# Attention and two MLPs on one core: each head pair's work put into two phases

## The chip, the cores and the metric

The kernel runs on one core of a Trainium2 chip. A core has five engines that run their own instruction lists in order: TensorE (PE; its weight loads are shown as PEld), VectorE (DVE), ScalarE (ACT), GpSimd (POOL) and SyncE (SP, which here only starts DMA transfers). TensorE writes its results to PSUM, of which this kernel uses eight banks; DVE and ACT read them from there. The metric is the device time of one execution in microseconds (us), lower is better.

## The reference

Attention over 4 batches and 12 heads (448 positions, 64 channels), then a squared-ReLU MLP and a gated MLP, each over 1792 tokens of width 768:

```python
def _attn_ref(q, k, v, g_q, g_k):
    q_n, k_n = (rmsnorm(q, g_q), rmsnorm(k, g_k))
    scores = scale * np.matmul(q_n, k_n.transpose(0, 1, 3, 2))
    scores = scores - np.max(scores, axis=-1, keepdims=True)
    attn = np.exp(scores)
    attn = attn / (np.sum(attn, axis=-1, keepdims=True) + 1e-09)
    return np.matmul(attn, v)
...
    x = attn_out.transpose(0, 2, 1, 3).reshape(B * S, H * D)
    h = np.maximum(x @ w_in, 0.0)          # 768 -> 2048
    x = h * h @ w_out                      # 2048 -> 768
    g = x @ w_gate                         # 768 -> 1536
    return (g / (1 + np.exp(-g)) * (x @ w_val)) @ w_out   # 1536 -> 768
```

The MLP weights come as 64-bit floats. The kernel reads them as pairs of 32-bit words and puts 32-bit floats together from them.

## The kernel before

**Attention** works on 24 pairs of heads. A pair's queries and keys are squared (`square`, ACT), summed (`sumsq`, DVE), turned into reciprocal roots (`rsqrt`) and normalised (`normalise`, POOL). `transposes` turns them on TensorE; ACT takes the high part of each value (L292) and DVE the remainder (`lows`), both into the tile `th`. The two heads of a pair lie in rows 0 to 63 and 64 to 127, so `maxpass` and `scores` are matmuls on 64 rows, one for each head. Positions go in four chunks of 112. `maxpass` multiplies the high parts alone, and DVE reduces the result to a maximum per query (L315). `negmax` transposes the four chunks of maxima into one tile `nm`. `scores` multiplies three times (high with high, high with low, low with high), adds the negative maxima by a fourth matmul, and ACT takes the exponential (L340, tile `p`). POOL adds chunks in pairs (`sg`, L343). `av` multiplies by V, `sums` sums the exponentials. Sums go to SBUF, are laid out anew by DMA (`sp`), inverted (`recip`, DVE), sent through DRAM to all rows (`row`, `rb`, SP), and `xnorm` multiplies the output by them into `x`.

The order is set by a table: each step is entered with a slot and a place in the slot (`at`), pairs are four slots apart, and the list is run sorted. A slot holds one chunk of scores of one pair, one maxpass chunk of a later pair, and whatever else is due. AV comes in two halves. PSUM is cut into three tiles of two banks for transposes, maxima and scores (`ps_s`), one bank for AV (`ps_a`), and one that sums and negmax share (`ps_n`).

**The MLPs** run in units: `up` (one block of 448 tokens, one slab of 128 hidden columns, 18 matmuls), `gateval` (two such) and `down` (36 matmuls). A value x weight product is three matmuls of high and low parts. Weight slabs are prepared step by step (`pieces`, six steps on DVE and ACT for each slab), and `prep(n)` runs n of them; `prep` is called from the attention table too. `split_x` cuts the attention output into high and low parts. `down` of a block follows one unit behind the `up` that ends its hidden block. `drain` holds the last reciprocals and multiplications, run in the first units.

Of the kernel before, what the change touches and what calls it, by code (L numbers as in the profile page):

```python
# [19 lines left out]
def kernel(  # L20
# [66 lines left out]
    state = {"load": 0, "prep": 0, "freed": 0, "half": None, "done": None, "cap": NEARLY}  # L87
# [5 lines left out]
    def load_slab():  # L93
        i = state["load"]
        if i >= len(slabs):
            return
        key, src = slabs[i]
        wide = src.dtype == I32
        if wide:
            t = mem["wraw"].tile([P, KD, 2 * P], I32, tag="raw", name="raw")  # L100
        else:
            t = mem["wraw"].tile([P, KD, P], F32, tag="raw", name="raw")
        nc.sync.dma_start(out=t, in_=src)
        raws[i] = t
        state["load"] += 1

# [6 lines left out]
    def pieces():  # L113
        for i, (key, src) in enumerate(slabs):
# [8 lines left out]
            else:  # L123
# [17 lines left out]
                load_slab()  # L141
# [8 lines left out]
            if raw.dtype != I32:  # L150
                load_slab()
# [15 lines left out]
    def split_x(t, ks=range(KD)):  # L167
        b0, n = blocks[t]
        for kk in ks:
            eng = nc.gpsimd if kk % 3 == 2 else nc.vector  # L170
            split(xs[t][:, 0, kk, :], xs[t][:, 1, kk, :], x[:, kk, b0:b0 + n], eng)

    def attention():
        with ExitStack() as late:
# [21 lines left out]
            mxz = [one_p.tile([CP, NCH, P], F32, tag=f"mxz{i}", name=f"mxz{i}") for i in range(2)]  # L196
# [6 lines left out]
            START = -18  # L203
            raw_t, qk_t, tp_t, xu_t, v_t, th_t, sq_t, ss_t, nm_t, p_t, sg_t, av_t, sp_t, rb_t = ({} for _ in range(14))
# [26 lines left out]
            def square(pi, j=None):  # L231
                if not ok(pi):
                    return
                if pi not in sq_t:
                    sq_t[pi] = nat.tile([CP, 2, NV, D], F32, tag="sq", name="sq")
# [14 lines left out]
            def rsqrt(pi, eng=None):  # L250
# [5 lines left out]
                e.tensor_scalar(out=ms, in0=ms, scalar1=1.0 / D, scalar2=1e-6, op0=ALU.mult, op1=ALU.add)  # L256
                nc.scalar.activation(out=u, in_=ms, func=AF.Ln)
                nc.scalar.activation(out=r, in_=u, func=AF.Exp, scale=-0.5)
                e.tensor_tensor(out=u, in0=r, in1=r, op=ALU.mult)
                e.tensor_tensor(out=u, in0=u, in1=ms, op=ALU.mult)  # L260
                e.tensor_scalar(out=u, in0=u, scalar1=-0.5, scalar2=1.5, op0=ALU.mult, op1=ALU.add)
                e.tensor_tensor(out=r, in0=r, in1=u, op=ALU.mult)
# [18 lines left out]
            def transposes(pi):  # L281
# [3 lines left out]
                th = th_t[pi] = th_p.tile([P, 4, S], F32R, tag="th", name="th")  # L285
                ps = ps_s.tile([P, 2, 512], F32, tag="s", name="s")
                for j in (1, 0):
                    for c in range(NCH):
                        nc.tensor.transpose(ps[:, j, c * CP:(c + 1) * CP], t[:, j, c], ident[:CP, :CP])  # L289
                tp_t[pi] = ps  # L290
                for j, gg, hi in ((1, gk, 0), (0, gq, 3)):
                    nc.scalar.activation(out=th[:, hi, :], in_=ps[:, j, :S], func=AF.Copy, scale=gg[:, 0:1])  # L292

            def lows(pi, j):
                if not ok(pi):
                    return
                ps, th = tp_t[pi], th_t[pi]
                gg, hi, li = ((gq, 3, 2), (gk, 0, 1))[j]
                nc.vector.scalar_tensor_tensor(
                    out=th[:, li, :], in0=ps[:, j, :S], scalar=gg[:, 0:1], in1=th[:, hi, :].bitcast(F32),  # L300
                    op0=ALU.mult, op1=ALU.subtract,
                )
# [3 lines left out]
            def maxpass(pi, c):  # L306
# [3 lines left out]
                ps = ps_s.tile([P, 2, 512], F32, tag="s", name="s")  # L310
# [4 lines left out]
                nc.vector.tensor_reduce(out=mxz[pi % 2][:, c, 0:P:D], in_=ps[:CP, :, :S], op=ALU.max, axis=AX.X)  # L315

            def negmax(pi):
                if not ok(pi):
                    return
                ps = ps_n.tile([P, 512], F32, tag="n", name="n")  # L320
                for c in range(NCH):
                    nc.tensor.transpose(ps[:, c * CP:(c + 1) * CP], mxz[pi % 2][:, c, :], ident[:CP, :CP])  # L322
                nm = nm_t[pi] = one_p.tile([P, S], F32R, tag="nm", name="nm", bufs=2)
                nc.scalar.activation(out=nm, in_=ps[:, :S], func=AF.Copy, scale=-1.0)

            def scores(pi, c):
# [3 lines left out]
                ps = ps_s.tile([P, 2, 512], F32, tag="s", name="s")  # L330
# [10 lines left out]
                if c % 2 == 1:  # L341
                    sg = sg_t[pi, c // 2] = p_p.tile([CP, 2, S], F32, tag="sg", name="sg", bufs=4)
                    nc.gpsimd.tensor_tensor(out=sg, in0=p_t[pi, c - 1], in1=p, op=ALU.add)  # L343


            def av(pi, c):
                if not ok(pi):
                    return
                if c == 0:
                    av_t[pi] = ps_a.tile([P, 512], F32, tag="av", name="av")  # L350
                p = p_t.pop((pi, c))
                for a, s in halves:
                    nc.tensor.matmul(  # L353
                        av_t[pi][s, :S], v_t[pi][:, a, c * D:(c + 1) * D], p[:, a, :],
                        start=(c == 0), stop=(c == NCH - 1),
                    )
                if c == NCH - 1:
# [276 lines left out]
```

## Time and profile before

| what | us |
|---|---|
| median of three runs (lowest, highest) | 1290.71 (1289.81, 1294.98) |
| the profiled execution | 1289.78 |
| its span, first to last instruction | 1288.0 |
| PE busy | 1264.1 (98%) |
| DVE, ACT, POOL busy | 820.5 (64%), 433.3 (34%), 288.4 (22%) |

The busy shares are means over two unlike halves: attention up to about 273 us, then the MLPs. A busy time on PE is the time with a matmul under way; matmuls overlap by their pipeline, so the cost of a block of matmuls is read from its start to the start of the next, not from its duration. An idle time in brackets behind a row is that of the engine just before it, with what ended it.

### The profile page before, as it was taken

How to read it: one execution, taken by the hardware profiler on the slowest of the kernel's cores; microseconds unless marked ns; L12 is line 12 of the kernel's file. 1: busy time of each engine (PE TensorE's matmuls, PEld its weight loads, DVE VectorE, ACT ScalarE, POOL GpSimd, SP SyncE). 2: the span in 40 equal slices, each digit the busy share in tenths (PEclk: the TensorE clock that was granted, in tenths of full speed). 3: DMA queues.
4: the chain of work that ended last, by engine and by line, in shares of the span. 5: the costliest groups of instructions: out<-in, count | busy, mean ns of one | idle time of the engine just before them, and what ended most of it. 6: DMA issues, size and time to landing. Idle time of an engine off the chain costs nothing.

```text
span 1288.0 us, 16575 instructions
## 1 busy us (share of the span) xinstructions
PE 1264.1 (98%) x6720; PEld 1059.1 (82%) x6720; DVE 820.5 (64%) x1151; ACT 433.3 (34%) x677; POOL 288.4 (22%) x258
## 2 busy tenths in 40 slices
PE   6999999999999999999999999999999999999998
PEld 3555555568989889898989899999999999999998
DVE  7777887766656565656565667475565664764634
ACT  5767777642322231313132442122121121221210
POOL 4666777632111120202020560000000000000000
PEclk9999999999999999999999999999999999999999
DMA  6233332130211121212021112021111120220013
GB/s 169 74 111 89 104 105 72 49 99 25 74 50 54 48 71 50 65 34 74 25 74 50 50 50 74 23 77 50 49 49 50 50 74 25 74 74 25 25 44 129
DMA packets 64830, 82.35 MB, mean 64 GB/s; under 512 B 8176, under 2 KB 61168, under 8 KB 64752
## 3 DMA queue, kind: packets, MB, share of 16 engines
q1 hardware_dynamic: 64752, 81.28, 20.1%
q8 instruction: 53, 0.87, 0.3%
q14 instruction: 25, 0.20, 0.0%
HBM read 75.50 MB, written 5.59 MB: 63 GB/s over the span
## 4 chain that ended last, share of the span: by engine, by line
PE 65%; issue 26%; POOL 6%; DVE 1%; ACT 1%; SPq 0%; DMA 0%; POOLq 0%; ACTq 0%
PE ps L499 29%; PE ps L547 17%; PE s L338 7%; PE av L353 6%; POOL s L521 5%; PE s L312 2%; PE s L289 2%; PE n L369 2%; PE n L322 1%; DMA raw<-in_q_dram 0%; SPq L220 0%; DVE mxz L315 0%; POOL sg L343 0%; DVE bits L134 0%; DVE hid L165 0%
## 5 line engine op out<-in xcount | busy, mean ns | idle before, releaser
L499 PE MATMUL ps<-xs,w 128*128 128x448 f32 x2880 | 599.8, 368 | 1.6 <-ACT sb L373 1.6
L499 PEld LDWEIGHTS ps<-xs,w 128*128 128x128 f32 x2880 | 542.5, 188 | 50.3 <-ACT sb L373 2.4
L547 PE MATMUL ps<-hid,w 128*128 128x448 f32 x2016 | 423.5, 367 | 5.8 <-ACT hid L164 3.2
L547 PEld LDWEIGHTS ps<-hid,w 128*128 128x128 f32 x2016 | 379.4, 189 | 41.2 <-ACT hid L164 6.2
L555 DVE TENSOR_TENSOR xacc<-ps,xacc 128x448 f32<-128x448 f32 x288 | 165.7, 617 | 47.7 <-PE ps L547 47.6
L165 DVE TENSOR_TENSOR hid<-s,hid 128x448 fp32r<-128x448 f32 x112 | 70.0, 625 | 157.8 <-ACT hid L164 157.6
L521 POOL TENSOR_TENSOR s<-s 128x448 f32<-128x448 f32 x64 | 76.0, 1188 | 364.0 <-ACT s L520 361.2
L164 ACT CAST hid<-s 128x448 fp32r<-128x448 f32 x112 | 63.5, 567 | 247.6 <-DVE s L534 159.4
L315 DVE TENSOR_REDUCE mxz<-s 112x2 f32<-112x896 f32 x96 | 103.8, 1084 | 34.5 <-PE s L312 34.2
L343 POOL TENSOR_TENSOR sg<-p 112x896 f32<-112x896 f32 x48 | 103.3, 2152 | 57.6 <-ACT p L340 57.6
L147 ACT CAST w<-bits 128x768 fp32r<-128x768 f32 x68 | 56.7, 834 | 156.6 <-DVE bits L143 156.6
L340 ACT ACTIVATE p<-s 112x896 f32<-112x896 f32 x96 | 86.7, 916 | 45.5 <-PE s L338 43.9
L338 PEld LDWEIGHTS s<-th 64*112 64x112 f32 x576 | 45.3, 174 | 54.9 <-issue 33.7
L149 DVE TENSOR_TENSOR w<-bits,w 128x768 fp32r<-128x768 f32 x68 | 65.7, 967 | 37.4 <-ACT w L147 36.2
L338 PE MATMUL s<-th 64*112 64x448 f32 x576 | 82.2, 391 | 0.9 <-ACT p L340 0.9
L353 PE MATMUL av<-p,v 112*64 112x448 f32 x384 | 82.8, 552 | 0.0
L530 ACT ACTIVATE s<-ps 128x448 f32<-128x448 f32 x48 | 26.1, 543 | 164.7 <-PE ps L499 164.7
L520 ACT ACTIVATE s<-ps 128x448 f32<-128x448 f32 x64 | 34.4, 538 | 132.9 <-PE ps L499 132.9
L132 ACT ACTIVATE w<-raw 128x768 fp32r<-128x768 f32 x68 | 61.5, 905 | 45.4 <-PE ps L547 45.4
L138 DVE SCALAR_TENSOR_TENSOR bits<-raw,bits 128x768 int32<-128x768 int32 x68 | 75.2, 1106 | 2.3
L531 DVE TENSOR_TENSOR s<-ps,s 128x448 f32<-128x448 f32 x48 | 29.8, 622 | 72.5 <-ACT s L530 72.5
L534 DVE TENSOR_TENSOR s<-ps,s 128x448 f32<-128x448 f32 x48 | 30.0, 624 | 71.9 <-PE ps L499 71.0
(56 smaller groups left out, 781.2 us busy)
## 6 DMA issues: line engine op xcount, KB each, us to landing
raw<-in_moe_w_out_dram SPq DMA_DIRECT2D x28, 768.0 KB
raw<-in_moe_w_in_dram SPq DMA_DIRECT2D x16, 768.0 KB
raw<-in_moe_w_gate_dram SPq DMA_DIRECT2D x12, 768.0 KB
raw<-in_moe_w_val_dram SPq DMA_DIRECT2D x12, 768.0 KB
raw<-in_k_dram SPq DMA_DIRECT2D x24, 224.0 KB
raw<-in_q_dram SPq DMA_DIRECT2D x24, 224.0 KB
v<-in_v_dram SPq DMA_DIRECT2D x24, 224.0 KB
rb<-row SPq DMA_DIRECT2D x48, 112.0 KB
```

The source lines that it names most:

```text
L138: nc.vector.scalar_tensor_tensor(out=bits, in0=lo, scalar=29, in1=bits, op0=ALU.logical_shift_right, op1=ALU.bitwise_or)
L149: nc.vector.tensor_tensor(out=t[:, 1, :], in0=src, in1=t[:, 0, :].bitcast(F32), op=ALU.subtract)
L165: (eng or nc.vector).tensor_tensor(out=dl, in0=src, in1=dh.bitcast(F32), op=ALU.subtract)
L315: nc.vector.tensor_reduce(out=mxz[pi % 2][:, c, 0:P:D], in_=ps[:CP, :, :S], op=ALU.max, axis=AX.X)
L338: nc.tensor.matmul(ps[:CP, a, :S], lhs, rhs, start=(w == 0), stop=(w == 3))
L340: nc.scalar.activation(out=p, in_=ps[:CP, :, :S], func=AF.Exp)
L343: nc.gpsimd.tensor_tensor(out=sg, in0=p_t[pi, c - 1], in1=p, op=ALU.add)
L353: nc.tensor.matmul(av_t[pi][s, :S], v_t[pi][:, a, c * D:(c + 1) * D], p[:, a, :], start=(c == 0), stop=(c == NCH - 1),)
L499: nc.tensor.matmul(ps[:, :n], w[:, wi, kk, :], xs[t][:, xi, kk, :], start=(mm == 0), stop=(mm == 3 * KD - 1))
L521: nc.gpsimd.tensor_tensor(out=s[:, :n], in0=s[:, :n], in1=s[:, :n], op=ALU.mult)
L547: nc.tensor.matmul(ps[:, :n], w[:, wi, o * P:(o + 1) * P], rhs, start=(mm == 0), stop=(mm == 5))
L555: nc.vector.tensor_tensor(out=a, in0=ps[:, :n], in1=a, op=ALU.add)
```

## The change

The table of slots is replaced by a loop over pairs. Iteration i first alternates, chunk by chunk, the maxima of pair i+1 with the scores of pair i; then come, in one stretch, the sums of i-1, the transposes of i+2, negmax of i+1 and all of AV of i. All of PSUM is one rotation of four two-bank tiles (`two_banks`); sums and negmax share a tile, in a bank each. The outer steps keep to this loop: `xnorm(i-3)` and the first additions of the reciprocal (`total(i-2)`, new) on POOL instead of DVE, one `normalise` half ahead of the chunks and one between them, squares and sums of squares of later pairs in the second phase. The gain vectors g_q and g_k are loaded from ACT's queue and multiplied together, so that keys need no scale. The last pair's exponentials are summed by TensorE without POOL's additions. Slab loads are collected and issued at the start of an iteration or unit (`load_slabs`). In the MLP, the square of `up` moves from POOL to DVE, the first three units run no slab steps, and the last splits of x are spread over seven units instead of five.

```diff
+    def load_slabs():
+        while state["want"]:
+            state["want"] -= 1
+            load_slab()
...
-            ps_s = late.enter_context(tc.tile_pool(name="ps_s", bufs=3, space=PSUM))
-            ps_a = late.enter_context(tc.tile_pool(name="ps_a", bufs=1, space=PSUM))
-            ps_n = late.enter_context(tc.tile_pool(name="ps_n", bufs=1, space=PSUM))
+            ps_p = late.enter_context(tc.tile_pool(name="ps_p", bufs=4, space=PSUM))
+
+            def two_banks():
+                return ps_p.tile([P, 2, 512], F32, tag="s", name="s")
...
+            def highs(pi):
+                if not ok(pi):
+                    return
+                nc.scalar.copy(th_t[pi][:, 0, :], tp_t[pi][1])
+                nc.scalar.activation(out=th_t[pi][:, 3, :], in_=tp_t[pi][0], func=AF.Copy, scale=gq[:, 0:1])
...
+            def total(pi):
+                if not ok(pi):
+                    return
+                sp = sp_t[pi]
+                nc.gpsimd.tensor_tensor(out=sp[:, 0, :], in0=sp[:, 0, :], in1=sp[:, 1, :], op=ALU.add)
+                nc.gpsimd.tensor_scalar(out=sp[:, 0, :], in0=sp[:, 0, :], scalar1=1e-9, scalar2=None, op0=ALU.add)
...
-                nc.vector.tensor_tensor(
+                nc.gpsimd.tensor_tensor(
                     out=x[:, hp, b * S:(b + 1) * S], in0=xu_t.pop(pi), in1=rb_t.pop(pi), op=ALU.mult
                 )
...
-                    nc.sync.dma_start(out=dst[half * D:(half + 1) * D, :], in_=src.rearrange("(d o) -> d o", o=1))
+                    nc.scalar.dma_start(out=dst[half * D:(half + 1) * D, :], in_=src.rearrange("(d o) -> d o", o=1))
...
+            for i in range(np_):
+                load_slabs()
...
+                elif i > 1:
+                    normalise(i + 3, None, (1, 2))
                 for c in range(NCH):
-                    at(F + c, 1, scores, pi, c)
-                    at(F + c - 7, 5.5, maxpass, pi, c)
-                    at(F + (2, 2, 4, 4)[c], 6, av, pi, c)
...
+                    maxpass(i + 1, c)
+                    scores(i, c)
+                    if c == 1:
+                        if i < np_ - 1:
+                            add(i, 0)
+                        if i > 1:
+                            normalise(i + 3, None, (0, 1))
+                        xnorm(i - 3)
+                        total(i - 2)
...
+                if i < np_ - 1:
+                    add(i, 1)
+                for pi in ((), (7, 8))[i] if i < 2 else (i + 7,):
+                    for j in (1, 0):
+                        load(pi, j)
...
+                if 10 <= i < 22:
+                    split_lo((i - 10) // 6, (i - 10) % 6)
+                if 2 <= i < 14:
+                    prep()
+                ps = two_banks()
+                sums(i - 1, ps[:, 0])
+                transposes(i + 2)
...
+                negmax(i + 1, ps[:, 1])
+                highs(i + 2)
+                negmax_out(i + 1, ps[:, 1])
+                sums_out(i - 1, ps[:, 0])
...
+                ps = two_banks()[:, 0]
+                av(i, ps)
+                load(i + 3, 2)
...
+                lows(i + 2, 1)
+                lows(i + 2, 0)
+                recip(i - 2)
+                for pi in squares.get(i, (i + 6,)):
+                    square(pi)
...
+                av_out(i, ps)
...
+                if i >= np_ - 2:
+                    prep(6)
+                if 9 <= i < 21:
+                    split_hi((i - 9) // 6, (i - 9) % 6)
...
-            nc.gpsimd.tensor_tensor(out=s[:, :n], in0=s[:, :n], in1=s[:, :n], op=ALU.mult)
+            nc.vector.tensor_tensor(out=s[:, :n], in0=ps[:, :n], in1=s[:, :n], op=ALU.mult)
...
-            prep(3 if phase == 0 else 4 if kind else 5)
+            load_slabs()
+            prep(0 if i < 3 else 3 if phase == 0 else 4 if kind else 5)
```

On PE, in the middle of attention, before: negmax, maxima, AV, scores and their maxima, maxima, transposes, sums.

```order
L322 MATMUL n<-ident,mxz_105 128x112 x4
L312 MATMUL s<-th 112x448 x2
L353 MATMUL av<-p,v 64x448 x4
L338 MATMUL s<-th 112x448 x6
L338 MATMUL s<-nm,ones 112x448 x2
L312 MATMUL s<-th 112x448 x2
L289 MATMUL s<-ident,qk 128x112 x8
L369 MATMUL n<-sg,onef 32x448 x4
```

The same engine and place with the change: the last chunk of scores, then sums (L400), transposes (L305), negmax (L344), AV (L379), and the next pair's first maxima and scores.

```order
L364 MATMUL s<-nm,ones 112x448 x2
L400 MATMUL s<-sg,onef 32x448 x4
L305 MATMUL s<-ident,qk 128x112 x8
L344 MATMUL s<-ident,mxz 128x112 x4
L379 MATMUL s<-p,v 64x448 x8
L335 MATMUL s<-th 112x448 x2
L364 MATMUL s<-th 112x448 x6
```

AV stands once with eight matmuls instead of twice with four, and the blocks between the scores have moved together.

On POOL, in the middle of attention, with the change: add, half a normalisation, the multiplication of the output (L435), the total (L417, L418), the second add, the other half.

```order
L370 TENSOR_TENSOR sg<-p 112x896
L287 TENSOR_TENSOR qk<-raw,r 112x2x4x64
L435 TENSOR_TENSOR xacc<-xu,rb 128x448
L417 TENSOR_TENSOR sp<-sp 56x16
L418 TENSOR_SCALAR sp<-sp 56x16
L370 TENSOR_TENSOR sg<-p 112x896
L287 TENSOR_TENSOR qk<-raw,r 112x2x4x64
```

L435, L417 and L418 are new on this queue; the second add now stands behind them. The counterparts before (L396, L382) were on DVE.

On ACT, at the end of attention, before: the last exponentials, the copy of the sums (L373), slab steps (L132, L147), the copy of AV (L359), then the first unit of the MLP (L520, L164).

```order
L340 ACTIVATE p<-s 112x896 x3
L373 COPY sb<-n 128x448
L147 CAST w_3217<-bits 128x768
L359 COPY xu<-av 128x448
L373 COPY sb<-n 128x448
L132 ACTIVATE w_3342<-raw 128x768
L520 ACTIVATE s<-ps 128x448
L164 CAST hid_3333<-s 128x448
L164 CAST xs_3340<-xacc 128x448 x3
```

With the change: two slab steps (L138, L153) of pair 22, the last four exponentials, the copies of sums (L408) and AV (L388), two slab steps, the last copy of sums, the first unit (L613, L170, L175).

```order
L138 ACTIVATE w_3203<-raw 128x768
L153 CAST w_3203<-bits 128x768
L366 ACTIVATE p<-s 112x896 x4
L408 COPY sb<-s 128x448
L388 COPY xu<-s 128x448
L138 ACTIVATE w_3288<-raw 128x768
L153 CAST w_3288<-bits 128x768
L408 COPY sb<-s 128x448
L613 ACTIVATE s<-ps 128x448
L170 CAST hid_3324<-s 128x448
L175 CAST xs_3331<-xacc 128x448
```

Slab steps now stand ahead of the last four exponentials and of the last copy of sums, and one split of x instead of three follows the first hidden block.

## Rows read from the trace of the kernel before

**Rows 1.** Stretches: start:end, length, busy us (instructions) of each engine, clock, DMA

```profile
120.00:160.00 40.00, 40.00 (x294) 21.02 (x290) 33.28 (x42) 30.20 (x48) 31.25 (x27) 1.00 0.30 88
240.00:280.00 40.00, 37.88 (x240) 20.02 (x239) 26.30 (x33) 21.84 (x32) 17.60 (x8) 0.96 0.25 76
280.00:300.00 20.00, 16.79 (x74) 14.67 (x73) 17.37 (x20) 10.06 (x19) 7.74 (x7) 0.91 0.27 91
400.00:500.00 100.00, 99.26 (x484) 90.47 (x483) 62.00 (x88) 26.40 (x42) 17.03 (x14) 1.00 0.17 56
```

**Rows 2.** Order of time, PE: start, us, engine, line, operation; one pair

```profile
89.14 0.60 PE L322 MATMUL n<-ident,mxz 112*128 112x112 f32 x4
89.67 0.45 PE L312 MATMUL s<-th 64*112 64x448 f32 x2
90.06 1.72 PE L353 MATMUL av<-p,v 112*64 112x448 f32 x8
91.71 0.87 PE L338 MATMUL s<-th 64*112 64x448 f32 x6
92.42 0.36 PE L338 MATMUL s<-nm,ones 64*112 64x448 f32 x2
92.62 0.37 PE L312 MATMUL s<-th 64*112 64x448 f32 x2
92.92 0.99 PE L289 MATMUL s<-ident,qk 112*128 112x112 f32 x8
93.83 0.96 PE L369 MATMUL n<-sg,onef 112*32 112x448 f32 x8
94.72 0.87 PE L338 MATMUL s<-th 64*112 64x448 f32 x6
...
98.49 0.37 PE L312 MATMUL s<-th 64*112 64x448 f32 x2
98.70 0.76 PE L338 MATMUL s<-th 64*112 64x448 f32 x6
99.30 0.36 PE L338 MATMUL s<-nm,ones 64*112 64x448 f32 x2
99.59 0.60 PE L322 MATMUL n<-ident,mxz 112*128 112x112 f32 x4
```

**Rows 3.** Order of time, PE, at the hand-over; in brackets idle before, releaser

```profile
273.13 16.66 PE L499 MATMUL ps<-xs,w 128*128 128x448 f32 x72 [1.60 <-ACT sb L373]
...
292.34 0.47 PE L547 MATMUL ps<-hid,w 128*128 128x448 f32 x1 [1.93 <-ACT hid L164]
294.08 8.28 PE L547 MATMUL ps<-hid,w 128*128 128x448 f32 x32 [1.28 <-DVE hid L165]
```

**Rows 4.** Order of time, SP queue and DVE, first microseconds

```profile
1.67 1.19 SPq L405 DMA_DIRECT2D gk<-in_g_k_dram  x2
...
11.53 0.68 DVE L299 SCALAR_TENSOR_TENSOR th<-s,gk,th 128x448 fp32r<-128x448 f32 x1
```

**Rows 5.** Groups by line and shape, 60 to 240 us: count, busy us, mean ns

```profile
L315 DVE TENSOR_REDUCE mxz<-s 112x2 f32<-112x896 f32 x70 | 75.8, 1083 | 26.8 <-PE s L312 26.7
L340 ACT ACTIVATE p<-s 112x896 f32<-112x896 f32 x69 | 62.3, 916 | 32.4 <-PE s L338 31.1
L343 POOL TENSOR_TENSOR sg<-p 112x896 f32<-112x896 f32 x35 | 73.7, 2107 | 37.8 <-ACT p L340 37.8
```

**Rows 6.** Order of time, POOL and DVE, last pair

```profile
267.74 2.79 POOL L343 TENSOR_TENSOR sg<-p 112x896 f32<-112x896 f32 x1 [1.27 <-ACT p L340]
...
268.69 2.66 DVE L143 SCALAR_TENSOR_TENSOR bits<-w,bits 128x768 f32<-128x768 f32 x1
```

**Rows 7.** Waits of the SP queue; order of time, DVE, last pairs

```profile
SPq L390 <- DMA row<-sp: 42.8, 24, 4.2
...
266.53 0.24 DVE L385 RECIPROCAL sp<-sp 56x16 f32<-56x16 f32 x1
...
271.57 0.63 DVE L396 TENSOR_TENSOR xacc<-xu,rb 128x448 f32<-128x448 f32 x1 [0.23 <-DMA rb<-row]
```

More of the change, by code (lines that the diff above doesn't have):

```diff
@@ L86 @@
     W = {}
-    state = {"load": 0, "prep": 0, "freed": 0, "half": None, "done": None, "cap": NEARLY}
+    state = {"load": 0, "prep": 0, "freed": 0, "half": None, "done": None, "cap": NEARLY, "want": 0}
     mem = {}
@@ L347, in av @@
+            def av(pi, ps):
                 if not ok(pi):
                     return
[L349 to L357, printed above, removed]
-                    xu = xu_t[pi] = rb_p.tile([P, S], F32, tag="xu", name="xu", bufs=3)
-                    nc.scalar.copy(xu, av_t.pop(pi)[:, :S])
@@ L362, in sums, with av_out @@
-            def sums(pi):
+                for c in range(NCH):
+                    p = p_t[pi, c]
+                    for a, s in halves:
+                        nc.tensor.matmul(
+                            ps[s, :S], v_t[pi][:, a, c * D:(c + 1) * D], p[:, a, :],
+                            start=(c == 0), stop=(c == NCH - 1),
+                        )
+            def av_out(pi, ps):
                 if not ok(pi):
                     return
-                ps = ps_n.tile([P, 512], F32, tag="n", name="n")
-                for w in range(2):
-                    for a in range(2):
-                        r0 = 32 * (2 * w + a)
-                        nc.tensor.matmul(
-                            ps[r0:r0 + 32, :S], onef, sg_t[pi, w][:, a, :], start=True, stop=True
-                        )
+                xu = xu_t[pi] = rb_p.tile([P, S], F32, tag="xu", name="xu", bufs=3)
+                nc.scalar.copy(xu, ps[:, :S])
@@ new lines, in sums @@
+            def sums(pi, ps):
+                if not ok(pi):
+                    return
+                last = (pi, 0) not in sg_t
+                for w in range(2):
+                    srcs = [p_t.pop((pi, 2 * w + c)) for c in range(2)] if last else [sg_t[pi, w]]
+                    for n, src in enumerate(srcs):
+                        for a in range(2):
+                            r0 = 32 * (2 * w + a)
+                            nc.tensor.matmul(
+                                ps[r0:r0 + 32, :S], onef, src[:, a, :], start=(n == 0), stop=(n == len(srcs) - 1)
+                            )
@@ L372, in sums, with sums_out @@
+            def sums_out(pi, ps):
+                if not ok(pi):
+                    return
                 sb = rb_p.tile([P, S], F32, tag="sb", name="sb")
@@ L462, in attention @@
[L462 to L473 removed]
+            normalise(0, nc.gpsimd, (0, 1))
@@ new lines, in attention @@
+            nc.vector.scalar_tensor_tensor(out=gq, in0=gq, scalar=SC, in1=gk, op0=ALU.mult, op1=ALU.mult)
+            sumsq(1)
+            transposes(0, True)
+            highs(0)
+            square(2)
+            rsqrt(1)
+            normalise(1)
+            for c in range(NCH):
+                maxpass(0, c)
+            square(3)
+            lows(0, 1)
+            lows(0, 0)
+            sumsq(2)
+            transposes(1)
+            highs(1)
+            n0 = two_banks()[:, 1]
+            negmax(0, n0)
```

215 lines of the change are left out of this document (109 added, 106 removed).

## The prediction

> **What bounds the kernel now.** I read the table of stretches first, then TensorE's instructions in order of time for one pair and for the hand-over from attention to the MLP, then the groups by line, and last the waits of the DMA queue. In the table [rows 1] the reader is to see that PE is busy for all 40.00 us of the stretch 120 to 160, and for 99.26 of 100 in the MLP stretch 400 to 500: TensorE sets the end in both halves, and the other engines have slack (DVE 33.28, ACT 30.20, POOL 31.25 of 40). The exception is the hand-over: 240:280 and 280:300 hold 37.88 and 16.79 us of PE work, at a mean granted clock of 0.96 and 0.91. So an edit counts if it shortens PE's own list in the attention half, if it fills the hand-over, or if it makes PE wait where today it never does.
>
> PE's list for one pair is [rows 2], a negmax at 89.14 to the next at 99.59: 10.45 us. Taken from start to next start, the blocks are negmax 0.53, max 0.39, AV 1.65, six score matmuls 0.71 and two with the maxima 0.20, max 0.30, transposes 0.91, sums 0.89, scores 0.71. The reader is to compare equal blocks with different neighbours. Six score matmuls take 0.60 at 98.70, behind a max of the same shape (64 rows), but 0.71 at 91.71 and 94.72, behind AV or sums (112 rows). A max takes 0.21 at 98.49, 0.30 at 92.62 where transposes follow, 0.39 at 89.67 between negmax and AV. The two with the maxima take 0.20, and 0.29 at 99.30 where negmax follows. So leaving the 64-row shape costs about 0.09 and coming back 0.10 to 0.11: 0.2 for an excursion. A pair makes four: negmax, AV, transposes with sums, AV again.
>
> **The change part by part.** *The pair.* Now four times max and scores, then sums, transposes, negmax and both halves of AV, one excursion. From the same rows: 4 x (0.21 + 0.60 + 0.20) = 4.04, leaving 0.09, sums 0.89, transposes 0.91, negmax 0.53, AV 2 x 1.65 = 3.30, return 0.11: 9.87. That is 0.58 less than 10.45. Below, 9.57: negmax beside transposes of the same shape could lose the 0.15 by which four in 0.53 exceed half of eight in 0.91, and AV in one piece another 0.15. I take 9.87. Pairs 1 to 21 run this full list: 21 x 0.58 = -12.2 us.
>
> *Does anything else hold the pair longer?* Reductions and exponentials come four in a row, with two score tiles and two max tiles in turn. The reduction takes 1.083, the exponential 0.916 [rows 5], PE's step is 1.01. A tile of scores is filled (0.80, and 0.16 for the last matmul to end: 0.36 long at 92.42, of which 0.20 is the step), then read for 0.92: 1.88 of the 2.02 before its turn returns. With 1.083 each, four reductions end 0.3 behind PE, and the sums behind them do not need the last. A stall of 0.1 in each pair would be +2, of 0.35 +7; I take 0. The maxima are needed by the next pair's scores, and AV's 3.30 stand between.
>
> *POOL.* It takes over the multiplication of the output by the reciprocal sums (half the columns of an add of 2.107 [rows 5]: about 1.05, my estimate) and two additions on 56x16. Its share today is 31.25 of 40 [rows 1], 8.16 per pair; with these about 9.5 of 9.87. It fits, with little left. What weighs against it: POOL and DVE hold each other up. A DVE step on 128x768 took 2.66 us, starting in an add of POOL that ended at 270.53 [rows 6]; its own time is what remains, 0.8. The Trainium skill ("SBUF — State Buffer", Who interferes with whom) says that a VectorE instruction with two SBUF inputs and a GpSimd instruction that reads SBUF exclude each other for a whole instruction; by that rule, more time on POOL means more waits on DVE, and the trace agrees. The edit also takes such an instruction off DVE, so DVE has left, per pair, one split or one weight step; DVE has 33.28 of 40 used, and a wait of 2.1 in a pair is covered. Cost 0, bound +7 as above.
>
> *The bounce through DRAM.* Recip, row, rb, output: 4.8 us from the end of the reciprocal (266.77) to 271.57 [rows 7]. SP now issues the row behind the V load, which waits for AV's end, at 9.8 of the pair. Landing then is near 14.5, 4.7 into the next pair; POOL comes to it after add and half a normalisation, at about 6.4 (exponential 1 ends near 3.1, then 2.1 and, for 512 of the add's 896 columns, an estimated 1.2). Hidden, with 1.6 to spare.
>
> *Start.* Two low parts of 0.68 [rows 4] leave the path to the first reductions, but the gain vectors' four loads, 1.19 for two, now stand on ACT ahead of the first squares. Bounds -3 (the path shorter, and the first pairs less ragged) to +2.4; I take -1.
>
> *Tail.* The last pair sums its exponentials on PE without POOL: eight matmuls for four, +0.9. On ACT, slab steps of pair 22 stand ahead of the last exponentials and wait for DVE; part of this stood there before. I take +1.5 together, from 0 to +5.
>
> *Hand-over.* The first MLP matmul waits 1.60 for ACT's copy of the last sums, then the first down projection waits 1.93 and 1.28 for its hidden block [rows 3]. The first wait stays: the first projection still follows that copy, itself behind a slab step. The other two come from a backlog on ACT, POOL and DVE: three slab steps and three splits per unit. No slab steps in units 0 to 2, one or two splits per unit and the square on DVE clear it: -3.2. There were two dips of the clock to the lower of its two levels: 0.04 x 40 = 1.6 and 0.09 x 20 = 1.8 us lost [rows 1]. The second begins with these waits, and I let it go with them: -1.7. Together -4.9, bounds -6 and 0.
>
> *The square on DVE in the MLP.* PE idles 0.74 of 100 us there [rows 1], so some 3 is the most that eight groups can win; DVE is at 62.00 of 100, and 64 x 0.6 more stay hidden. I take -0.7; bounds -3 and +3 (a slab step in front of a square).
>
> **Sum.** -12.2 - 1 + 1.5 - 4.9 - 0.7 = -17.3. The profiled execution took 1289.78 (span 1288.0, and 1.78 around it), which gives 1272.5; it is 0.9 under the median of the three runs, 1290.71, well inside their spread. I say 1272.
>
> **The rivals.** *The excursion's cost returns inside the stretch.* Sums, transposes and AV load 32, 128 and 64 columns; if each of the three changes between them cost a whole 0.2, the pair is at 10.47 and the 12 us are gone: 1284. For it: four negmax transposes take 0.53, more than half of eight. Against: transposes directly before sums, today's one such border, take 0.91 for eight, 0.114 each, where the four of negmax take 0.13 each. The Trainium skill ("TensorEngine Tiling (Array Packing)", Key Properties) has it that a change of tiling mode, unlike a change of tile, drains TensorE; by that rule these borders pay too, as in this rival, and the trace shows it only at the borders with 64 rows.
>
> *The alternating phase waits* for exponentials or reductions, because ACT or DVE comes late into the pair (squares, splits and slab steps stand ahead). For it: 1.88 of 2.02 leaves ACT 0.14. Against: either engine catches up 0.1 per step or has 1.5 to 2 us free per pair. At 0.3 per pair: 1272 + 6 = 1278.
>
> *The other side: the chain of divisions closes on itself.* Output i-3 stands on POOL ahead of the total of i-2, its reciprocal waits for the total, the bounce for the reciprocal, and the next output for the bounce. Its round is 1.05 + 0.4 + 0.24 + 4.8 = 6.5 us. With the longest wait of a broadcast for its row, 4.2 against a mean of 42.8/24 = 1.8 [rows 7], it is about 9. It decides from 9.87; slower than 1290.7 from 10.8. With the bounce twice as long, 9.6, a pair takes 11.3: 1272 + 21 x 1.4 = 1301. Against it: the V load stands in the same queue before, and the weight slabs come in few pairs.
>
> **How the numbers follow.** Forecast 0.70 (own range 1263 to 1277), waiting phase 0.15, cost returns 0.10, closed chain 0.05. The range of 1262 to 1284 takes in 9.57 per pair at one end (-6.3, and some of the start) and the first two rivals, or a hand-over without gain, at the other. Faster by over 0.5%, about what a measurement of this kernel can tell from no change, is below 1284.3: all of the forecast and the waiting phase, half of the returned cost, 0.89. Within 0.5%: 0.06. Slower, above 1297: 0.05.
>
> **What would show it.** The step from one negmax to the next near 9.9, PE without idle time in 120:160; scores at 0.60 in all four places; a first down projection that waits less than 0.5 us; one dip of the clock instead of two; POOL near 95% in attention without DVE or PE waiting for it. A step of 10.3 or more, waits of PE for exponentials or reductions, or of POOL for rb, would make it wrong.

## The result and the profile after

The changed kernel takes 1273.4 us (median of four executions, 1271.36 to 1277.07), the kernel before beside it 1292.66: a ratio of 0.9855, 95% interval 0.9819 to 0.9891. The prediction was 1272 in a range of 1262 to 1284. The profiled execution took 1271.36, its span is 1269.6; before it was 1289.78 and 1288.0, so the two traces differ by 18.4 us.

The table of stretches, with the columns of [rows 1]:

```profile
120.00:160.00 40.00, 39.21 (x304) 22.30 (x303) 31.70 (x40) 30.85 (x50) 37.73 (x38) 1.00 0.38 109
240.00:280.00 40.00, 35.42 (x206) 24.59 (x203) 22.71 (x29) 18.42 (x31) 14.86 (x16) 0.96 0.22 68
280.00:300.00 20.00, 18.36 (x89) 16.38 (x88) 16.24 (x22) 7.35 (x13) 6.69 (x5) 1.00 0.24 79
400.00:500.00 100.00, 99.61 (x487) 90.99 (x486) 67.44 (x103) 24.75 (x39) 0.00 (x0) 1.00 0.17 55
```

POOL went from 31.25 to 37.73 of 40 us in the attention, 94%. PE now idles there, 0.79 of 40, which it did not before. In 280:300 the granted clock is back at 1.00; one dip is left, in the first half of the second row.

PE in order of time, one pair that waits for nothing (start, us, engine, line, operation), against [rows 2]:

```profile
98.42 0.46 PE L335 MATMUL s<-th 64*112 64x448 f32 x2
98.71 0.76 PE L364 MATMUL s<-th 64*112 64x448 f32 x6
99.31 0.37 PE L364 MATMUL s<-nm,ones 64*112 64x448 f32 x2
...
101.79 0.85 PE L364 MATMUL s<-th 64*112 64x448 f32 x6
102.46 0.39 PE L364 MATMUL s<-nm,ones 64*112 64x448 f32 x2
102.78 0.96 PE L400 MATMUL s<-sg,onef 112*32 112x448 f32 x8
103.67 0.99 PE L305 MATMUL s<-ident,qk 112*128 112x112 f32 x8
104.49 0.55 PE L344 MATMUL s<-ident,mxz 112*128 112x112 f32 x4
104.97 3.23 PE L379 MATMUL s<-p,v 112*64 112x448 f32 x16
108.12 0.47 PE L335 MATMUL s<-th 64*112 64x448 f32 x2
```

From 98.42 to 108.12 are 9.70 us, where the pair of before took 10.45. From start to next start: sums 0.89 as before, transposes 0.82 instead of 0.91, negmax 0.48 instead of 0.53, AV 3.15 instead of 2 x 1.65. The scores take 0.60 behind the first maximum and 0.67 behind the last.

Groups by line and shape, 60 to 240 us, POOL, against [rows 5] (count, busy us, mean ns, idle before):

```profile
L370 POOL TENSOR_TENSOR sg<-p 112x896 f32<-112x896 f32 x37 | 79.3, 2143 | 8.7 <-ACT p L366 7.0
L435 POOL TENSOR_TENSOR xacc<-xu,rb 128x448 f32<-128x448 f32 x18 | 20.9, 1161 | 1.7 <-DMA rb<-row 1.7
```

The product takes 1.16 us on POOL (estimated at 1.05) and over its 18 runs waited 1.7 us in all for its broadcast.

PE in pair 22, which has no transposes left, and then at the hand-over, against [rows 3]; in brackets idle before and releaser:

```profile
241.25 0.96 PE L400 MATMUL s<-sg,onef 112*32 112x448 f32 x8
242.14 0.60 PE L344 MATMUL s<-ident,mxz 112*128 112x112 f32 x4
242.67 3.23 PE L379 MATMUL s<-p,v 112*64 112x448 f32 x16
...
251.75 0.96 PE L400 MATMUL s<-sg,onef 112*32 112x448 f32 x8 [2.43 <-ACT p L366]
252.63 4.92 PE L379 MATMUL s<-p,v 112*64 112x448 f32 x16
...
261.37 14.86 PE L592 MATMUL ps<-xs,w 128*128 128x448 f32 x72 [2.15 <-ACT sb L408]
276.06 7.46 PE L640 MATMUL ps<-hid,w 128*128 128x448 f32 x36
...
298.21 0.47 PE L592 MATMUL ps<-xs,w 128*128 128x448 f32 x1 [0.60 <-ACT xs L175]
299.72 8.04 PE L592 MATMUL ps<-xs,w 128*128 128x448 f32 x38 [1.04 <-POOL xs L179]
```

In pair 22 negmax stands directly behind sums and takes 0.53, where behind transposes, of its own shape, it took 0.48. The MLP begins at 261.37 instead of 273.13 (-11.8 us) and takes 1008.2 instead of 1014.9 us (-6.6). The first down projection no longer waits. The 72 projections ahead of it take 14.86 instead of 16.66 us, because no dip of the clock lies on them. The dip that is left follows PE's 2.43 us of idle time and makes the last AV 4.92 instead of 3.23 us, since part of it ran at 1.2 instead of 2.4 GHz (granted clock 0.91 over 240:260).

### The profile page after: what moved, and what is told of

Its sections match the earlier page's. It is cut to its first block, busy times and chain, and to the rows that moved or that the text cites. A ratio compares the mean times of both kernels' runs of the same rounds, so it can differ in the third digit from the quotient of the medians.

```text
span 1269.6 us, 16772 instructions
## 1 busy us (share of the span) xinstructions
PE 1244.7 (98%) x6728; PEld 1060.1 (84%) x6728; DVE 828.0 (65%) x1167; ACT 433.2 (34%) x679; POOL 251.1 (20%) x268
## 4 chain that ended last, share of the span: by engine, by line
PE 81%; DVE 8%; ACT 4%; POOL 2%; DMA 2%; issue 2%; SPq 0%; ACTq 0%; POOLq 0%
PE ps L592 37%; PE ps L640 31%; PE s L364 5%; PE s L379 4%; PE s L305 1%; PE s L335 1%; ACT hid L170 1%; DVE hid L171 1%; DVE s L614 1%; PE s L400 1%; DVE bits L149 1%; DVE w L155 1%; ACT w L153 1%; POOL qk L287 1%; POOL sg L370 1%
## 5 line engine op out<-in xcount | busy, mean ns | idle before, releaser
L170 ACT CAST hid<-s 128x448 fp32r<-128x448 f32 x112 | 63.5, 567 | 242.8 <-DVE s L627 160.9
L338 DVE TENSOR_REDUCE mxz<-s 112x2 f32<-112x896 f32 x96 | 101.0, 1092 | 23.2 <-PE s L335 22.5
L171 POOL TENSOR_TENSOR xs<-xacc,xs 128x448 fp32r<-128x448 f32 x24 | 29.0, 1246 | 419.1 <-ACT xs L170 419.1
L153 ACT CAST w<-bits 128x768 fp32r<-128x768 f32 x68 | 56.7, 834 | 155.0 <-DVE bits L149 155.0
L370 POOL TENSOR_TENSOR sg<-p 112x896 f32<-112x896 f32 x46 | 98.7, 2147 | 12.9 <-ACT p L366 11.0
L364 PE MATMUL s<-th 64*112 64x448 f32 x576 | 77.8, 375 | 2.3 <-ACT xu L388 2.1
L379 PE MATMUL s<-p,v 112*64 112x448 f32 x384 | 79.2, 556 | 0.0
L138 ACT ACTIVATE w<-raw 128x768 fp32r<-128x768 f32 x68 | 61.7, 907 | 49.6 <-PE ps L640 47.8
L627 DVE TENSOR_TENSOR s<-ps,s 128x448 f32<-128x448 f32 x48 | 30.0, 625 | 73.6 <-PE ps L592 72.8
L613 ACT ACTIVATE s<-ps 128x448 f32<-128x448 f32 x64 | 34.7, 542 | 126.1 <-PE ps L592 126.0
L624 DVE TENSOR_TENSOR s<-ps,s 128x448 f32<-128x448 f32 x48 | 29.9, 623 | 72.8 <-ACT s L623 72.8
L614 DVE TENSOR_TENSOR s<-ps,s 128x448 f32<-128x448 f32 x64 | 39.7, 620 | 47.7 <-ACT s L613 47.7
L149 DVE SCALAR_TENSOR_TENSOR bits<-w,bits 128x768 f32<-128x768 f32 x68 | 66.1, 972 | 6.7 <-ACT w L138 3.8
```

Of the source, the lines that this page charges most:

```text
L149: nc.vector.scalar_tensor_tensor(out=src, in0=t[:, 0, :].bitcast(F32), scalar=1.178e-9, in1=src, op0=ALU.is_ge, op1=ALU.mult)
L170: nc.scalar.copy(dh, src)
L171: (eng or nc.vector).tensor_tensor(out=dl, in0=src, in1=dh.bitcast(F32), op=ALU.subtract)
L338: nc.vector.tensor_reduce(out=mxz[:, c, 0:P:D], in_=ps[:CP, :, :S], op=ALU.max, axis=AX.X)
L364: nc.tensor.matmul(ps[:CP, a, :S], lhs, rhs, start=(w == 0), stop=(w == 3))
L370: nc.gpsimd.tensor_tensor(out=sg, in0=p_t[pi, 2 * w], in1=p_t[pi, 2 * w + 1], op=ALU.add)
```

## The experiments

Each run is compared with the kernel before on the same chip; the changed kernel stands at 1273.4 and 0.9855. The kernel before had medians of 1290.7 to 1292.7 beside them, so a difference of 1 to 3 us between two edits is not clear of noise; where the text leans on one, it leans on the rows.

| run | us, median | ratio to before, 95% |
|---|---|---|
| rows112 | 1287.71 | 0.9961 (0.9947 to 0.9974) |
| rows64 | 1275.49 | 0.9867 (0.9837 to 0.9897) |
| phases_apart | 1300.88 | 1.0062 (1.0038 to 1.0085) |
| root_behind | 1271.52 | 0.9833 (0.9815 to 0.9850) |
| tail_order | 1270.45 | 0.9847 (0.9829 to 0.9864) |
| prep_in_units | 1274.02 | 0.9876 (0.9853 to 0.9900) |
| square_pool | 1274.71 | 0.9877 (0.9862 to 0.9893) |
| xnorm_dve | 1369.99 | 1.0609 (1.0583 to 1.0635) |
| xnorm_dve_late | 1277.11 | 0.9900 (0.9885 to 0.9915) |
| best_xu4 | 1265.12 | 0.9800 (0.9786 to 0.9813) |
| best_dve | 1272.85 | 0.9860 (0.9845 to 0.9875) |
| best_sums_early | 1268.26 | 0.9821 (0.9801 to 0.9840) |

**What an excursion costs: rows112 and rows64.** One small matmul in front of three maxima of each pair, of 112 rows in one kernel and of 64 in its control:

```
 def maxpass(pi, c):
     ps = two_banks()
+    if c:
+        nc.tensor.matmul(ps[:32, 0, S:512], ones[:CP, :32], ones[:CP, :64], start=True, stop=True)
```

> Leaves the result as it is; adds one small matmul of 112 rows in front of the maxima of key chunks 1, 2 and 3 of each pair, into columns of the maxima's tile that nobody reads: 72 in all. Theory (the change of row count itself costs TensorE about 0.2 us each time it goes out to 112 rows and back to 64): the next matmul of 64 rows starts late by what it starts late behind AV, so 72 x about 0.2 to 0.25 = 14 to 18 us more than the same kernel with 64-row matmuls in the same place, a pair's step 0.6 to 0.75 us longer. Rival (the gaps of the kernel before came from waiting tiles and operands, and the row count costs nothing): both kernels agree within 2 us.

> The control of the run before: the same 72 small matmuls in the same places, with 64 rows like their neighbours. Both theories: 72 x about 0.05 us of their own, some 3 to 5 us over the changed kernel (about 1277).

PE in order of time, rows112 and then rows64:

```profile
105.13 0.38 PE L366 MATMUL s<-nm,ones 64*112 64x448 f32 x2
105.44 0.22 PE L335 MATMUL s<-ones 112*32 112x64 f32 x1
105.58 0.46 PE L337 MATMUL s<-th 64*112 64x448 f32 x2
105.88 0.79 PE L366 MATMUL s<-th 64*112 64x448 f32 x6
```

```profile
101.83 0.38 PE L366 MATMUL s<-nm,ones 64*112 64x448 f32 x2
102.03 0.19 PE L335 MATMUL s<-ones 64*32 64x64 f32 x1
102.05 0.44 PE L337 MATMUL s<-th 64*112 64x448 f32 x2
102.25 0.86 PE L366 MATMUL s<-th 64*112 64x448 f32 x6
```

From the start of the matmuls with the maxima to the next scores it is 0.75 in the one and 0.42 in the other: in this place leaving costs 0.11 and returning 0.22. An undisturbed pair takes 10.62 against 9.88, so three excursions add 0.74, 0.25 each on the mean. The medians differ by 12.2 us, less than 24 x 0.74 = 17.8 and than the 14 to 18 that were expected, because the longer pair hides the stalls that the control has in pairs 3, 5, 11, 13, 15 and 17 (its steps run from 9.87 to 11.16, those of rows112 are 10.6 in all but two of pairs 1 to 21). The row count costs time by itself; the first theory holds, at a smaller total. It is not the only change of shape that costs: see the section on why the prediction was right.

**The alternation undone: phases_apart.**

```
 for c in range(NCH):
     maxpass(i + 1, c)
+for c in range(NCH):
     scores(i, c)
```

> Undoes the alternation alone: the four maxima of the next pair are issued first, then the four scores, in the same four tiles and with the same stretch of sums, transposes and AV behind. Theory (the alternation hides VectorE's reductions, 1.04 us each, and ScalarE's exponentials, 0.92 us each, beside each other): PE now waits for reductions before the scores, whose tiles they free one by one; the phase grows from about 4.3 us to 0.3 + 1.05 x 4 + 0.6 + the part of the last exponential that AV waits for, some 0.8 to 1.2 us a pair and 18 to 28 us in all, 1291 to 1301. Rival (the gain lies in the one stretch, and four tiles hide either order): within 4 us of 1273.

PE and then DVE, in order of time:

```profile
107.53 1.21 PE L335 MATMUL s<-th 64*112 64x448 f32 x8
109.19 0.87 PE L364 MATMUL s<-th 64*112 64x448 f32 x6 [0.44 <-DVE mxz L338]
...
107.90 0.24 DVE L424 RECIPROCAL sp<-sp 56x16 f32<-56x16 f32 x1 [1.48 <-POOL sp L418]
108.07 4.06 DVE L338 TENSOR_REDUCE mxz<-s 112x2 f32<-112x896 f32 x4
```

The pair grows to 10.81, 1.11 over 9.70: PE issues four maxima in 1.21 us and then follows the reductions, 4.06 for four. The one stretch without the alternation would have made the kernel slower than before, by 0.4 to 0.85%.

**The long pairs: root_behind.** In the changed kernel pairs 2, 3, 5, 11, 13, 15 and 17 take 10.0 to 10.9 us instead of 9.7. Rows of one of them, in order of time, ACT, PE and POOL:

```profile
127.94 0.23 ACT L270 ACTIVATE u<-ss 112x32 f32<-112x32 f32 x1 [1.85 <-POOL ss L268]
...
129.28 0.51 ACT L388 COPY xu<-s 128x448 f32<-128x448 f32 x1
...
129.85 0.86 PE L364 MATMUL s<-th 64*112 64x448 f32 x6 [0.78 <-ACT xu L388]
...
127.69 0.22 POOL L268 TENSOR_SCALAR ss<-ss 112x32 f32<-112x32 f32 x1
```

ACT waits 1.85 for a small operation on the late POOL, copies AV's output 1.7 us after AV's end, and the scores that reuse that tile wait. The edit moves the logarithm and the exponential behind the copy:

```
-if i > 1 and i % 2 == 0:
-    rsqrt(i + 4, part=1)
 ...
 av_out(i, ps)
+if i > 1 and i % 2 == 0:
+    rsqrt(i + 4, part=1)
```

> Moves one thing: the logarithm and exponential of the reciprocal root, in every second pair, go behind the copy of AV's output on ScalarE instead of in front of the square. Theory (in these pairs ScalarE waits up to 1.8 us for GpSimd's scaling of the sums, so it copies AV's output late, and the scores of chunk 1 that reuse that tile wait up to 1.2 us): the steps of 10.0 to 10.9 us become 9.7, the sum over the pairs falls by about 4 us, and the time by 3 to 4 us to about 1269.5; the PE waits for the copy (2.1 us as the profile names them) are gone. Rival (the odd steps come from GpSimd itself, whose busy share is 94%, and only show there): same time within 1 us, PE waits elsewhere, at the sums or at the transposes.

The waits of pairs 3, 5 and 11 go (9.66, 9.64, 9.79), but two steps of 11.0 come, where the copy waits 2.24 us for POOL in another way: its buffer, one of three, is free only once POOL has multiplied the output of three pairs before. 1.9 us by the medians, half of what was expected, and the intervals overlap.

**Late slab steps: tail_order.**

```
 if 2 <= i < 14:
     prep()
+elif i == np_ - 1:
+    prep(2)
 ...
 if i >= np_ - 2:
-    prep(6)
+    prep(4)
 ...
 sums_out(np_ - 1, ps)
+prep(2)
```

> Moves only the twelve late slab steps: of the slab that was prepared between pairs 22 and 23, the last two steps go behind the last exponentials; of the next slab the last two go behind the last copy of the sums. Theory (ScalarE's rounding of the slab waits 2.6 us for VectorE in front of the four last exponentials and again in front of the last copy, so PE stands still for 2.4 us, its granted clock falls, and the projections begin late): the four exponentials start at about 247 instead of 250.7, no PE wait in front of the last AV but for 0.5 us, projections start 4 to 5 us earlier (256.5 to 257.5 us instead of 261.4), time 1268.5 to 1269.5. Rival (the slabs or the last x are what the projections really wait for): the start of the projections moves, but the gain comes back as waits of the first down projection or of the second half's up projections, time within 1.5 us of 1273.

PE at the same place as above:

```profile
252.76 0.96 PE L400 MATMUL s<-sg,onef 112*32 112x448 f32 x8
253.65 3.23 PE L379 MATMUL s<-p,v 112*64 112x448 f32 x16
...
259.20 14.86 PE L595 MATMUL ps<-xs,w 128*128 128x448 f32 x72 [0.67 <-ACT sb L408]
```

The idle time in front of AV and the dip on it are gone; from the last scores on, the projections begin 5.7 us earlier (9.9 us behind AV of the pair before, against 15.5). But this execution had lost 3.5 us in its pairs, and the dip came back at 280 to 320 us (0.95 and 0.96), at the waits for the late split of x. By the medians it is 3.0 us, by the ratios 1.0, and the intervals overlap: the rows show the shorter tail, the gain in the whole time is not shown.

**Slab steps back in the first units: prep_in_units.**

```
-prep(0 if i < 3 else 3 if phase == 0 else 4 if kind else 5)
+prep(3 if phase == 0 else 4 if kind else 5)
```

> Undoes one part: three slab steps in each of the first three MLP units, as the kernel before had them. Theory (the steps on VectorE and ScalarE between the units delay the hidden values, which the first down projection waits for): the waits of 1.9 and 1.3 us of the kernel before come back at the first down projection in part, 1 to 3 us slower. Rival (the waits of the kernel before came from the split of x for the later blocks and from the GpSimd lock): same time within 0.7 us.

```profile
260.58 16.42 PE L592 MATMUL ps<-xs,w 128*128 128x448 f32 x72 [2.16 <-ACT sb L408]
279.87 0.47 PE L640 MATMUL ps<-hid,w 128*128 128x448 f32 x1 [2.27 <-ACT hid L170]
280.53 6.87 PE L640 MATMUL ps<-hid,w 128*128 128x448 f32 x32 [0.19 <-DVE hid L171]
```

The first wait for the hidden block returns, 2.27 us (1.93 before), so the slab steps were its cause. Of the second, 1.28 before, only 0.19 returns: its cause lies elsewhere, in the square or in the splits of x. With the square back on POOL (next run) this block takes 7.84 instead of 7.46; the splits were not tested apart. The median moves by 0.6 only, within the interval: the waits for x, 0.60 and 1.04 in the changed kernel, are gone in exchange. The 16.42 of the projections (a dip of the clock) is no mark of this edit: root_behind, with the units of the changed kernel, has 16.41 there.

**The square back on POOL: square_pool** (line 614 as it was, `nc.gpsimd`, of s with itself).

> Undoes one part: the square of the up projection goes back to GpSimd. Theory: it lies off the path except where the down projection waits for it, so 0.7 us slower, PE busy 99.3 instead of 99.6 of 100 us in the window 400 to 500. Rival (GpSimd's slower square also lengthens VectorE's operations beside it, and the first hand-over waits for it): 2 to 4 us slower.

PE is busy 99.23 of 100 us in 400:500. Over 320:720 that is 397.3 instead of 398.6 us of work, 1.3 us, the same as the medians' 1.3. The intervals overlap, so the time alone does not show it; the equal medians may be chance.

**The product on VectorE: xnorm_dve and xnorm_dve_late.** First line 435 alone, then also its place:

```
-nc.gpsimd.tensor_tensor(out=x[...], in0=xu, in1=rb, op=ALU.mult)
+nc.vector.tensor_tensor(out=x[...], in0=xu, in1=rb, op=ALU.mult)
```

```
 total(i - 2)                # xnorm(i - 3) was here, in the alternating phase
 ...
 recip(i - 2)
+xnorm(i - 3)                # xnorm_dve_late only
```

> Undoes one part: the product of AV's output with the reciprocals goes back from GpSimd to VectorE. Theory (GpSimd is busy 94% in the attention, and that lateness reaches PE through ScalarE in every second pair): GpSimd falls to about 83%, VectorE takes about 0.65 us a pair more, the late pairs get shorter, time 1 to 3 us faster than 1273. Rival (VectorE is itself near the limit, with the reductions in the alternating phase, and the product waits there for the broadcast of the reciprocals, in front of reductions): slower by up to 0.5 us a pair, 1275 to 1285.

> The product of AV's output with the reciprocals on VectorE again, but issued behind the residues and the reciprocal of the stretch instead of between the reductions of the alternating phase; nothing else differs from the changed kernel. Theory (the 97 us of the run with the product on VectorE come from the place: there it stands in front of reductions and waits 3.7 us in each pair for the broadcast of reciprocals that were issued one pair before, and this closes a ring of reciprocal, transfer, product, maxima, reciprocal; on VectorE as such it costs 0.62 us, which fits into the time that VectorE waits in the stretch): pairs of 9.7 to 10 us, GpSimd at about 84% instead of 94%, 1269 to 1273 us. Rival (VectorE cannot carry the product): pairs of 10.3 us and more, over 1285.

DVE and then PE of xnorm_dve in order of time; below them DVE and POOL of xnorm_dve_late:

```profile
90.54 0.23 DVE L424 RECIPROCAL sp<-sp 56x16 f32<-56x16 f32 x1
93.15 2.11 DVE L338 TENSOR_REDUCE mxz<-s 112x2 f32<-112x896 f32 x2 [2.38 <-PE s L335]
98.90 0.74 DVE L435 TENSOR_TENSOR xacc<-xu,rb 128x448 f32<-128x448 f32 x1 [3.64 <-DMA rb<-row]
99.56 2.08 DVE L338 TENSOR_REDUCE mxz<-s 112x2 f32<-112x896 f32 x2
...
100.69 1.69 PE L305 MATMUL s<-ident,qk 112*128 112x112 f32 x8 [2.57 <-DVE mxz L338]
```

```profile
128.62 0.56 DVE L435 TENSOR_TENSOR xacc<-xu,rb 128x448 f32<-128x448 f32 x1
138.93 1.87 DVE L435 TENSOR_TENSOR xacc<-xu,rb 128x448 f32<-128x448 f32 x1
...
138.21 2.10 POOL L370 TENSOR_TENSOR sg<-p 112x896 f32<-112x896 f32 x1
```

The first closes a ring: the product waits 3.64 us for a broadcast whose reciprocal ended 8.1 us before, two reductions stand behind it, and behind those the next reciprocal. Of pairs 4 to 21 eleven take 14.1 to 14.6 us and seven 15.7 to 16.9; neither the theory nor the rival of this run came near that. Not all of it is waiting. In each of these pairs PE waits 2.6 us or more, and then the granted clock is at its lower level (1.2 GHz) for 3.4 us, in the seven for 6.8; the eight transposes behind the wait above take 1.49 to the next start instead of 0.82. So of the 4.4 us that an ordinary pair has over 9.70, 2.6 are the wait and 1.7 the clock. This is the third rival of the prediction, on another engine: on POOL the same broadcast has landed before POOL comes to it (idle 2.1 us in all over 40:250). In the second the ring is open and 92.9 of the 96.6 us are back, so the place cost them, not the engine. But 3.7 us remain by the medians, against my expectation; the intervals just overlap, but in the traces pairs 1 to 21 take 4.0 us more than in the changed kernel. Beside an add of POOL the product takes 1.87 instead of 0.56 us, and the copy of AV's output waits for it, 2.15 us behind this one.

**Versions from the findings: best_xu4, best_dve, best_sums_early.** best_xu4 joins root_behind and tail_order, gives the copy a fourth buffer (`tag="xu", bufs=4`), and splits x two by two in units 0 to 5. best_dve has three buffers and the product of xnorm_dve_late. best_sums_early is best_xu4 with `total(i - 2)` ahead of the normalisation, the product behind it, and the split in the loop one pair later.

> A version from the findings: the logarithm and exponential of the root behind the copy of AV's output, a fourth buffer for that copy (it waits for the product of three pairs before, on the late GpSimd), the late slab steps behind the last exponentials and the last copy, and the split of x for the last block one MLP unit earlier. Theory: no step over 9.9 us from pair 4 on (3 to 4 us less), projections begin at about 255.5 us, the two waits of 0.6 and 1.0 us before the last up projections go (with the clock's fall behind them): 1264 to 1267. Rival (GpSimd's share remains the limit): steps over 10 us remain at the sums or transposes, 1268 to 1271.

> As the run before, but with three buffers and the product on VectorE behind the reciprocal of the stretch, which takes 1.16 us a pair from GpSimd. Theory (GpSimd's lateness is the root of the long pairs): 1263 to 1266, at or below the version that leaves the product on GpSimd. Rival (the product's place on VectorE delays the square's and reductions' chain or the copy of AV's output): above the other by 2 us and more.

> The best version so far, with GpSimd's total of the sums issued in front of its normalisation instead of behind it and the product, and the split of x in the loop one pair later. Theory (in the three remaining long pairs, 11.0, 10.7 and 11.0 us, an add on GpSimd takes 4.5 instead of 2.1 us while VectorE runs the split and a slab step back to back; then VectorE's reciprocal waits up to 3.3 us for the late total, in front of the reductions that the maxima's tiles wait for): the reciprocal no longer waits, these pairs fall to 9.7 to 10.2 us, the time by 2.5 to 3.5 us to about 1262. Rival (GpSimd is late whatever the order, and the late normalised keys or sums reach PE at the transposes or sums): within 1 us of 1265.

best_xu4 is the fastest that is settled: 1265.1, its interval wholly below that of the changed kernel. The waits for x are gone and none of the stretches from 120 to 160 and from 200 to 320 us has a clock under 1.00. From pair 4 on three long pairs remain (11.0, 10.7, 11.0). POOL, DVE and PE of the first, in order of time:

```profile
132.26 4.49 POOL L370 TENSOR_TENSOR sg<-p 112x896 f32<-112x896 f32 x1
...
139.40 0.24 DVE L424 RECIPROCAL sp<-sp 56x16 f32<-56x16 f32 x1 [3.31 <-POOL sp L418]
...
140.65 0.46 PE L335 MATMUL s<-th 64*112 64x448 f32 x2 [1.17 <-DVE mxz L338]
```

An add on POOL takes 4.49 instead of 2.1 us while DVE runs a sum of squares, a split, a slab step and two residues back to back; the total behind it is late, DVE's reciprocal waits 3.31 for it, and reductions and maxima follow. best_dve, with the product on DVE, takes 1272.9, 7.7 more than best_xu4, and most of its pairs take 10.1 to 11.0: its rival came true, not its theory that POOL's lateness is the root of the long pairs.

best_sums_early shows what the order is worth and does not deliver it: its profiled execution took 1260.81, every pair from 4 to 21 took 9.6 to 9.8 us, but the other four took 1265.17 to 1269.33, and the median, 1268.26, misses the 1262 that were expected. The trace is that of the fastest of five, so it cannot show where the others lost their time. That stays open.

## Why the prediction was right

By its own steps, against the traces. The start is read from the first maxima behind the first AV, before and with the change:

```profile
31.23 0.45 PE L312 MATMUL s<-th 64*112 64x448 f32 x2
28.82 0.46 PE L335 MATMUL s<-th 64*112 64x448 f32 x2
```

The steps:

- *The pair, 9.87 instead of 10.45.* Right in mechanism but too narrow, and near in size because two errors cancel. The undisturbed pair takes 9.70: negmax, transposes and AV came out 0.05, 0.09 and 0.15 cheaper, part of them up to the bound; the scores of the last two chunks take 0.05 and 0.07 more than 0.60, for which no run here shows the reason. That alone would be 21 x 0.75 = -15.8 instead of -12.2. From the start of pair 1 (28.82) to the end of pair 21 (236.89) the mean is 9.91, so stalls take 4.4 back and -11.4 is left.
- *Nothing else holds the pair longer: taken at 0.* Wrong. 208.07 us for 21 pairs are 4.4 over 21 x 9.70. The step that failed says that POOL "fits, with little left": at 94%, predicted near 95, its lateness reached PE through ACT's copy, and seven of the 21 pairs took 10.0 us or more. The rival of the waiting phase named the right effect and, in the main, the wrong gate: of PE's waits that the trace names, four (2.1 us) were for the tile of AV's output and one (0.13) for an exponential. The other half of the 4.4 shows no idle time, and its gate stays open.
- *The bounce* is hidden as predicted, but for 1.7 us in 18 products; xnorm_dve shows what lies behind that margin.
- *Start and tail.* The first AV of before ends at 31.2, now 28.8: -2.4, inside the bounds and more than the -1 taken; no run takes the start apart. The remainder, from the end of pair 21 to the MLP, is 24.5 us; before it was 273.13 - 31.2 - 21 x 10.45 = 22.5. So +2.0 instead of +1.5, and tail_order, where the tail is 5.7 us shorter, shows why: the slab steps ahead of the last exponentials and of the last copy.
- *The hand-over, -4.9.* The waits of 1.93 and 1.28 are gone (-3.2), and both blocks that ran under a lower clock are shorter: 16.66 to 14.86, and 32 matmuls of the down projection 8.28 to 6.6, -3.5 together. The new waits for x, which the prediction did not have, take back 1.6: -5.1. That this is so near -4.9 is luck: one of the two dips, counted as gone here, only moved into the last AV, and the tail's +2.0 pays 1.7 for it; with both at their own places it is -3.4 for the hand-over and +0.3 for the tail. prep_in_units confirms the cause of the first wait, not of the second.
- *The square, -0.7.* Measured -1.3 by busy time.
- *The cost does not return inside the stretch.* It comes to no more than was counted, but not because these borders are free: a change of columns alone costs too, and the block prices of the sum had it in them. In [rows 2] eight transposes take 0.91 and four of negmax 0.53. That is 0.095 for each, with 0.15 left over for the borders of either block, although the transposes end at sums, a change of columns alone (128 to 32, both with 112 rows). With the change the two blocks, of one shape, stand side by side: 0.82 and 0.48, 1.30 for twelve, and about 0.15 is left for both together. Directly behind sums negmax takes 0.53 again. So the prediction misread this border when it set 0.114 for each of eight against 0.13 for each of four: one fixed price was spread over eight and over four. A pair before changes the shape of its matmuls nine times, now four times; 0.75 for five of them is 0.15 each. The Trainium skill has it that a change of tiling mode drains TensorE ("TensorEngine Tiling (Array Packing)", Key Properties); the trace agrees for rows (0.25 there and back) and, at 112 rows, for columns (about 0.15). In rows64, however, a matmul of 32 columns among those of 112, all on 64 rows, shows no such price: 0.20, 0.02 and 0.20 from start to start. Why that one is free stays open.
- *POOL and DVE hold each other up.* 0.56 and 1.87 for one product, 2.1 and 4.49 for one add. The Trainium skill ("SBUF — State Buffer", Who interferes with whom) calls it an exclusive lock, held for a whole instruction. The trace agrees for the product, which ends 0.5 us behind the add. It does not explain the add: that is 2.4 us longer than usual, and none of the five DVE operations beside it lasts more than 1.21.

These come to -11.4 - 2.4 + 2.0 - 5.1 - 1.3 = -18.2, of the 18.4 between the traces; -17.3 was predicted.

## What to carry to other kernels

Where TensorE sets the end, look at equal blocks with different neighbours: a change of a matmul's shape, of rows and at 112 rows of columns too, is a cost that no wait shows, and putting blocks of one shape side by side saves it. It pays only if the other engines' work still alternates beside it; here the order inside the phase was worth more (27 us) than the whole change. An engine at 94% is not slack: follow what its small operations release, and keep short operations that others wait for ahead of its long ones.

## What was not expected of the hardware

- One instruction in the wrong place of an in-order queue cost 96.6 us, 7.6%, with its own time at 0.6 to 0.7 us in most pairs: it closed a ring that took 8.1 us from reciprocal to use, and the waits in it came with the lower clock, 3.4 us and more in every pair from 4 to 21.
- An add on POOL that takes 2.1 us can take 4.5 while DVE runs five short operations in a row, so the hold-up can outlast one instruction of the other engine.
- Twelve transposes pay for their borders once when they stand together (1.30) and twice when they stand apart (0.91 and 0.53), though no row shows PE idle.
- The dip of the clock moved rather than vanished: at 240:260 (0.91) around PE's wait of 2.43 us in the changed kernel, at 280:320 in tail_order, around waits of 0.61 and 1.05 us; best_xu4, without these waits, shows none from 200 to 320 us. In xnorm_dve each pair from 4 to 21 has both, a wait of 2.6 us or more and a dip behind it. That the waits cause it was not tested apart.
